# Third and fourth blocks of w3 and w_out converted as four units of 512 columns instead of two of 1024

## The chip, the cores and the metric

The program runs on one core of a Trainium2 chip. What counts is the device time of one execution in microseconds (us). The kernel before was timed three times: 809.39, 810.38 and 811.29 us, median 810.38 us. One further execution was recorded by the profiler; its own time was 810.48 us, and all rows below come from it.

## What is computed

The reference is a chain of a windowed attention and two layers on its result (2304 tokens, 512 wide). All inputs arrive as 64-bit floats.

```python
attn = softmax(mask(q @ k.T / 8, window=64)) @ v          # 4 x 8 heads, 576 tokens, 64 wide
x = attn as (2304, 512)
a = x @ w1;  b = x @ w2                                   # 512 -> 1024
h = (a * b) @ w3                                          # w3: 1024 x 1024
x = h @ w_out                                             # w_out: 1024 x 512
g = leaky(x @ w_in);  out = g @ w_out2                    # 512 -> 2048 -> 512
```

## The kernel before

The chip has no 64-bit floats, so every weight is loaded as raw words and turned into 32-bit floats on the core. One piece of a weight that goes through this is called a **unit** here. The list `units` (filled by `unit`, L503) holds them in the order in which they are loaded and converted. A unit passes through five steps, each one or two instructions:

1. load: SP starts a DMA into a raw buffer (`load_unit`, L418);
2. scale: ACT scales the high words (L455) and takes three low bits out of the low words (`low_bits`, L427);
3. shift: DVE shifts the high words and joins the low bits (L483);
4. bits: DVE puts the sign in (`sign`, L432). At this point the raw buffer is free, and `feed` may start the load of a later unit, whose field `after` says how many units must have passed this step;
5. fin: for a weight that is used as it is (w_out, w1, w2), `store` makes two parts of it: ACT rounds it into a high part (L357) and DVE or POOL subtracts that for the low part (L368 on DVE for the first w_out blocks, L361 on POOL for the third and fourth slot, L366 on POOL for w1 and w2). For w3 nothing is computed; its words wait in `words`.

`advance` does one such step for several units at a time, which makes a software pipeline; `until(n, ...)` runs it until n units are finished.

The first phase of the program multiplies w3 by w_out once, so that later only one matrix is needed (`wf`). The loop over `its` goes through 16 blocks: two halves `gi` of w3's rows, and in each eight blocks `l` of 128 columns. For each block PE transposes four 128 x 128 pieces of w3 (`w3_tr`, L517; the result is read out by ACT, L519, and DVE, L520, into the tile `w3T`), and multiplies them with block `l` of w_out (`w3_mm`: three products for each of four 128 x 512 results, L77, L78, L79, written into `mm`). `w3_tr` runs two blocks ahead of `w3_mm`. At the end of a half the four results are read out into `wf` (L540 on ACT, L541 on DVE).

The attention of the first chunk of tokens is interleaved with this phase, by slot numbers (`plan_att`, `slot`): loads of q, k and v (L670), transposes of k and q on PE (L235) with a read-out of k by ACT (`kT`, L242) and of q by DVE (`qbd`, L254), scores (L268), softmax (L272 on DVE, L276 on ACT, L284 and L285 on DVE, L286 on POOL), the transposes of the weights (L299, read out by ACT, L302) and the products with v (L331), which ACT and DVE read out into `x` (L334, L335). The tile `pa`, into which L235 and L331 both write, has one buffer, so a transpose of the next k waits until DVE's L335 has read the products.

The order on each engine is fixed when the program is built. A scheduler places the instructions by its own estimate of times, with priorities; small differences in the units change where it puts them. On the chip each engine works through its list in order.

Units before: 0 to 3 are w3 block 0, w_out block 0, w3 block 1, w_out block 1, each of 512 columns (512 KB). All others have 1024 columns (1024 KB): units 4 and 5 are blocks 2 and 3 of w3 together and of w_out together, and so on. Raw buffers are four slots of `raw_all`, and two tiles borrowed from `wf` (`wf_raw`).

Of the kernel before, what the change touches and what calls it, by code (L numbers as in the profile page):

```python
# [21 lines left out]
def tile_kernel(ctx: ExitStack, tc: tile.TileContext, q, k, v, w1, w2, w3, w_out, w_in, w_out2, out):  # L22
# [18 lines left out]
    P = 128  # L41
# [4 lines left out]
    KF = DFF // P  # L46
# [12 lines left out]
    UC = 512  # L59
# [9 lines left out]
    def f32(ap):  # L69
        return ap.bitcast(F32)  # L70

    def first():

        return tc.high_priority(offset=3000)
# [153 lines left out]
    def load(ls):  # L228
        for dst, src in ls:
            sp.dma_start(dst, src)  # L230
# [106 lines left out]
    def wslot(key):  # L337
        pl, tag, bufs = wpool, "w", 8
        if key[0] == "wo2":
            pl, tag, bufs = (po1, "w1", 4) if key[1] < 4 else (po2, "w2", 4)  # L340
        elif key[0] == "wf":
            tag, bufs = "wf", 4
        return pl.tile([P, 2, 2 * UC], F32R, name=tag, tag=tag, bufs=bufs)
# [7 lines left out]
    def store(key, half):  # L351

        def fin(f):
            if key not in slots:
                slots[key] = wslot(key)
            t, sl = slots[key], slice(0, 2 * UC) if half is None else slice(UC * half, UC * half + UC)
            act.copy(t[:, 0, sl], f)  # L357
            if key in (("wo", 2), ("wo", 3)):
                for i in range(2):
                    si = slice(UC * i, UC * i + UC)  # L360
                    pool.tensor_tensor(out=t[:, 1, si], in0=f[:, si], in1=f32(t[:, 0, si]), op=ALU.subtract)  # L361
                return
            if key[0] in ("w1", "w2"):
                for i in range(0, 2 * UC, 512):
                    si = slice(i, i + 512)
                    pool.tensor_tensor(out=t[:, 1, si], in0=f[:, si], in1=f32(t[:, 0, si]), op=ALU.subtract)  # L366
                return
            dve.tensor_tensor(out=t[:, 1, sl], in0=f, in1=f32(t[:, 0, sl]), op=ALU.subtract)  # L368
        return fin

    units = []
    last = {}
# [124 lines left out]
    def until(n, stop):  # L497
        while n_of["fin"] < n:
            was = dict(n_of)
            advance(stop)  # L500
            assert n_of != was

    def unit(src, fin, key, at=None, after=0, f_at=None):  # L503
        used = [(key[1], key[2] + j) for j in range(f_at[1])] if key[0] == "w3" else []
        units.append({"src": src, "fin": fin, "at": at, "after": after, "f_at": f_at,
                      "free": lambda: not any(x in words for x in used)})
        last[key] = len(units)
# [5 lines left out]
    def w3_tr(f):  # L513
        t = p0.tile([P, 2, 4, P], F32R, name="w3T", tag="w3T", bufs=2)
        ps = ps_ab.tile([P, 4, P], F32, name="ab", tag="ab")
        for i in range(4):
            pe.transpose(ps[:, i, :], f[:, i], ident)  # L517
        both = t.rearrange("p s i k -> p s (i k)")
        pss["act"] = act.copy(both[:, 0], ps.rearrange("p i k -> p (i k)")).ins  # L519
        pss["dve"] = dve.tensor_tensor(out=both[:, 1], in0=ps.rearrange("p i k -> p (i k)"), in1=f32(both[:, 0]),  # L520
                                       op=ALU.subtract).ins
        w3T.append(t)

    def w3_mm(gi, l, half):
        t = w3T[0]
        wo = rows2(slots["wo", l // 2])
        for i in range(2 * half, 2 * half + 2):
            if l == 0:
                wps[i] = ps_mm.tile([P, DM], F32, name="mm", tag="mm")
            mm3(wps[i], t[:, 0, i, :], t[:, 1, i, :], wo[:, 0, l % 2], wo[:, 1, l % 2], l == 0, l == KF - 1)  # L530
        if half == 0:
            return
        w3T.pop(0)
        if l == KF - 1:
            for i in range(2):
                if ("wf", 2 * gi + i) not in slots:
                    slots["wf", 2 * gi + i] = wslot(("wf", 2 * gi + i))
            for i in range(4):
                wf = rows2(slots["wf", 2 * gi + i // 2])
                act.copy(wf[:, 0, i % 2], wps[i])  # L540
                dve.tensor_tensor(out=wf[:, 1, i % 2], in0=wps[i], in1=f32(wf[:, 0, i % 2]), op=ALU.subtract)  # L541

    words = {}

    def wide_w3(gi, l):

        def fin(f):
            for j in range(2):
                words[gi, l + j] = f.rearrange("p (k j m) -> p k j m", j=2, m=P)[:, :, j]
        return fin  # L550

    def raw_at(i, n):
        return lambda: raw_all[:, i:i + n].rearrange("p n m -> p (n m)")
# [3 lines left out]
    def wf_raw(i):  # L557

        def at():
            if i not in spare_raw:  # L560
                spare_raw[i] = wpool.tile([P, 2 * UC], I64, name="wf", tag="wf", bufs=4)
            return spare_raw[i]
        return at

    for l in range(2):
        unit(w3[0:4 * P, P * l:P * l + P].rearrange("(k p) m -> p k m", p=P), (lambda l: lambda f: words.update({(0, l): f.rearrange("p (k m) -> p k m", m=P)}))(l),
             ("w3", 0, l), raw_at(2 * l, 1), 0, (2 * l, 1))
        unit(w_out[P * l:P * l + P, :], store(("wo", 0), l), ("wo", l), raw_at(2 * l + 1, 1), 0, (2 * l + 1, 1))
    PLACES = [wf_raw(0), wf_raw(1), raw_at(0, 2), raw_at(2, 2)]
    AFTER = {4: 0, 5: 0, 6: 2, 7: 4}  # L570
    for gi in range(2):
        for l in range(2 if gi == 0 else 0, KF, 2):
            i = len(units)
            unit(w3[4 * P * gi:4 * P * gi + 4 * P, P * l:P * l + 2 * P].rearrange("(k p) m -> p k m", p=P), wide_w3(gi, l),
                 ("w3", gi, l), PLACES[i % 4], AFTER.get(i, i - 3), (2 * (i % 2), 2))
            if gi == 0:
                i = len(units)
                unit(w_out[P * l:P * l + 2 * P, :].rearrange("(k p) m -> p k m", p=P), store(("wo", l // 2), None),
                     ("wo", l), PLACES[i % 4], AFTER.get(i, i - 3), (2 * (i % 2), 2))
    W12 = len(units)  # L580
    for p in range(KD):
        for w, name in ((w1, "w1"), (w2, "w2")):
            i = len(units)
            unit(w[:, 2 * P * p:2 * P * p + 2 * P].rearrange("(k p) m -> p k m", p=P), store((name, p), None), (name, p),
                 PLACES[2 + i % 2], i - 3 if i < W12 + 2 else i - 1, (2 * (i % 2), 2 if p else 0))
    PHASE_B = len(units)

    def keep(i):
# [54 lines left out]
    def slot():  # L643

        for _, n, _, f in sorted(ev.pop(clock["t"], []), key=lambda e: e[:2]):
            with ExitStack() as how:
                if f in (av, qk, tr) and clock["t"] >= PACED_FROM:
                    how.enter_context(tc.issue_after(pss["last"]))
                if f is prep_k and n > NHP or f is prep_q and n > 2 * NHP + 1:
                    how.enter_context(tc.issue_after(pss["dve"]))  # L650
                how.enter_context(tc.high_priority(offset=100))
                f(n)
        clock["t"] += 1
# [5 lines left out]
    def start_loads(i):  # L659

        if i in (W12 + 1, W12 + 2, W12 + 3):
            dma.append(pss["load"])
            for ls in held.pop(len(dma) - 1, []):
                with tc.issue_after(pss["load"]):
                    load(ls)
        for _ in range(0 if i < 5 else 1 if i < 10 else 7):
            if todo_qkv:
                dst, src = todo_qkv.pop(0)
                with tc.issue_after(pss["load"]), first():
                    pss["load"] = sp.dma_start(dst, src).ins  # L670
# [14 lines left out]
    for i, (gi, l) in enumerate(its):  # L685
        w3_mm(gi, l, 0)
        if i + 2 < len(its):
            g2, l2 = its[i + 2]
            if l2 % 2 == 0:
                until(last["w3", g2, l2], W12 + 2 if i >= 10 else W12)  # L690
            w3_tr(words.pop((g2, l2)))
            if l2 % 2 and g2 == 0:
                until(last["wo", l2 - 1], W12)
        for at, n in ((13, 1), (15, 2)):
            if i == at:
                until(W12 + n, W12 + 2)
        slot()
        w3_mm(gi, l, 1)
        slot()
# [220 lines left out]
    for c in range(NC):  # L920
        for i in range(3 * KF):
            f, part = divmod(i, 3)
# [357 lines left out]
```

## Time and profile before

| | |
|---|---|
| time of the three timed runs | 809.39, 810.38, 811.29 us; median 810.38 us |
| time of the profiled execution | 810.48 us |
| its span from the first to the last instruction | 808.7 us |
| mean granted clock of PE over the span | 0.998 of full speed |
| PE busy | 784.8 us (97%) |
| PE weight loads busy | 725.0 us (90%) |
| DVE busy | 560.8 us (69%) |
| ACT busy | 433.0 us (54%) |
| POOL busy | 71.4 us (9%) |

PE is the tensor engine, DVE the vector engine, ACT the scalar engine, POOL the general engine, SP the one that starts most DMAs. A busy time counts from the start of an instruction to its end. Since matmuls overlap, PE's busy share says only where PE has nothing at all to do. The granted clock is the share of full speed (2.4 GHz) that PE was given; 0.50 is 1.2 GHz.

### The profile page before, as it was taken

Reading aid. Unit: us, or ns where it says so; the run is one execution under the profiler, and the core shown is the slowest. Engines: PE = TensorE matmul, PEld = TensorE weight load, DVE = VectorE, ACT = ScalarE, POOL = GpSimd, SP = SyncE. Lnnn points to the kernel's source line nnn. Section 1 sums busy time; section 2 is a strip of 40 time slices with the busy share of each in tenths; the row PEclk is TensorE's granted clock in tenths of the full one; section 3 lists DMA queues with packets and bytes.
Section 4 is the critical chain, followed back from the end, with each engine's and each line's share of the span. In section 5 each row is a group of like instructions: output and inputs, shape, how many; then the busy total and the mean of one; then the engine's idle time right before and its main releaser. Section 6 shows DMA issues by size and latency. Waiting matters only on the chain.

```text
span 808.7 us, 14587 instructions
## 1 busy us (share of the span) xinstructions
PE 784.8 (97%) x5156; PEld 725.0 (90%) x5156; DVE 560.8 (69%) x1343; ACT 433.0 (54%) x968; POOL 71.4 (9%) x73
## 2 busy tenths in 40 slices
PE   5898999999999999999999999999999999999997
PEld 4776899999988888888788999999999999999997
DVE  6977676276446448884812865867668999898976
ACT  7885774244233325443511754654457867575744
POOL 1314244011011101110000000000000000000000
PEclk9999999999999999999999999999999999999999
DMA  9986374346646467894500557889998754444321
GB/s 338 301 252 160 103 204 113 82 114 150 158 109 166 102 157 197 261 292 160 180 8 1 170 191 272 287 320 338 319 314 285 216 166 135 128 139 130 111 92 53
DMA packets 184409, 147.12 MB, mean 182 GB/s; under 512 B 117904, under 2 KB 143760, under 8 KB 184336
## 3 DMA queue, kind: packets, MB, share of 16 engines
q1 hardware_dynamic: 181312, 141.34, 58.4%
q10 hardware_dynamic: 3024, 4.85, 1.6%
q8 instruction: 40, 0.66, 0.3%
q14 instruction: 33, 0.27, 0.1%
HBM read 98.96 MB, written 47.19 MB: 181 GB/s over the span
## 4 chain that ended last, share of the span: by engine, by line
PE 79%; DMA 7%; DVE 4%; SPq 3%; ACT 2%; issue 1%; POOL 0%; DVEq 0%; ACTq 0%; POOLq 0%
PE o L78 7%; PE o L79 7%; PE o L77 7%; PE pr L77 7%; PE pr L78 7%; PE pr L79 7%; PE ab L77 6%; PE ab L78 6%; PE ab L79 6%; PE mm L77 4%; PE mm L78 4%; PE mm L79 4%; PE sc L268 3%; SPq L230 3%; PE pa L331 2%; DMA wd<-f 2%
## 5 line engine op out<-in xcount | busy, mean ns | idle before, releaser
L77 PE MATMUL ab<-x,w 128*128 128x512 f32 (+1 forms) x320 | 119.6, 376 | 0.8 <-ACT a L719 0.8
L79 PE MATMUL ab<-x,w 128*128 128x512 f32 (+1 forms) x320 | 118.9, 371 | 0.0
L78 PE MATMUL ab<-x,w 128*128 128x512 f32 (+1 forms) x320 | 118.5, 370 | 0.0
L77 PE MATMUL pr<-yop,w 128*128 128x384 f32 x300 | 101.2, 337 | 1.0 <-ACT c L875 1.0
L79 PE MATMUL pr<-yop,w 128*128 128x384 f32 x300 | 101.0, 337 | 0.0
L78 PE MATMUL pr<-yop,w 128*128 128x384 f32 x300 | 100.9, 336 | 0.0
L875 ACT COPY c<-pr 128x384 f32<-128x384 f32 x95 | 45.2, 480 | 64.5 <-PE pr L79 55.9
L276 ACT ACTIVATE s<-s,nm 128x128 f32<-128x128 f32 x144 | 56.4, 395 | 39.3 <-DVE nm L272 38.8
L78 PE MATMUL o<-yop,yop 128*128 128x256 f32 x259 | 72.9, 282 | 0.0
L723 DVE TENSOR_TENSOR ab<-ab,a 128x512 f32<-128x512 f32 (+1 forms) x40 | 25.7, 642 | 68.2 <-PE ab L79 46.9
L79 PE MATMUL o<-yop,yop 128*128 128x256 f32 x259 | 72.9, 282 | 0.0
L77 PE MATMUL o<-yop,yop 128*128 128x256 f32 x259 | 72.9, 281 | 0.0
L77 PEld LDWEIGHTS ab<-x,w 128*128 128x128 f32 x320 | 60.1, 188 | 9.6 <-ACT a L719 1.5
L79 PEld LDWEIGHTS ab<-x,w 128*128 128x128 f32 x320 | 60.1, 188 | 8.0
L78 PEld LDWEIGHTS ab<-x,w 128*128 128x128 f32 x320 | 60.1, 188 | 7.6
L878 DVE TENSOR_TENSOR c<-pr,c 128x384 f32<-128x384 f32 x74 | 41.0, 555 | 29.9 <-PE pr L79 16.7
L1017 ACT CAST yop<-raw 128x256 fp32r<-128x256 f32 (+1 forms) x92 | 42.4, 485 | 35.6 <-PE o L78 34.2
L286 POOL TENSOR_TENSOR s<-s,rs 128x512 f32<-128x512 f32 (+1 forms) x40 | 39.5, 988 | 242.0 <-DVE rs L285 193.0
L78 PE MATMUL mm<-ab,wf 128*128 128x512 f32 (+1 forms) x160 | 60.4, 377 | 0.0
L79 PE MATMUL mm<-ab,wf 128*128 128x512 f32 (+1 forms) x160 | 59.5, 372 | 0.0
L77 PEld LDWEIGHTS pr<-yop,w 128*128 128x128 f32 x300 | 56.3, 188 | 1.7 <-ACT c L875 1.6
L724 ACT CAST ab<-ab 128x512 fp32r<-128x512 f32 (+1 forms) x40 | 21.7, 544 | 67.0 <-DVE ab L723 66.7
(148 smaller groups left out, 1981.4 us busy)
## 6 DMA issues: line engine op xcount, KB each, us to landing
hd<-c SPq DMA_DIRECT2D x96, 192.0 KB, 4.5
raw<-hd SPq DMA_DIRECT2D x32, 512.0 KB, 3.7
raw<-in_moe_w_dram SPq DMA_DIRECT2D x11, 1024.0 KB, 5.6
raw<-in_moe_w_out_dram SPq DMA_DIRECT2D x18, 512.0 KB, 5.0
raw<-in_moe_w_in_dram SPq DMA_DIRECT2D x16, 512.0 KB, 5.3
wd<-f SPq DMA_DIRECT2D x32, 256.0 KB, 4.3
raw<-wd SPq DMA_DIRECT2D x30, 256.0 KB, 4.8
pd<-tb SPq DMA_DIRECT2D x12, 512.0 KB, 2.8
```

The source lines that it names most:

```text
L77: pe.matmul(ps, lhsT=lh, rhs=rh, start=first, stop=False, skip_group_check=more)
L78: pe.matmul(ps, lhsT=lh, rhs=rl, start=False, stop=False, skip_group_check=more)
L79: return pe.matmul(ps, lhsT=ll, rhs=rh, start=False, stop=last, skip_group_check=more).ins
L230: sp.dma_start(dst, src)
L268: pe.matmul(sc[:, t, :], lhsT=qb[:, t, :], rhs=kT[n][:, k0:k0 + P], start=True, stop=True)
L276: act.activation(out=s[:, t, :], in_=s[:, t, :], func=AF.Exp, bias=nm[:, t:t + 1], scale=-1.0, accum_out=sm[:, t:t + 1])
L286: pool.tensor_tensor(out=s[:, 0:m], in0=s[:, 0:m], in1=rs[:, 0:m].unsqueeze(2).to_broadcast([P, m, P]), op=ALU.mult)
L723: dve.tensor_tensor(out=ps, in0=ps, in1=pss["a"], op=ALU.mult)
L724: pss["act"] = act.copy(t[:, 0], ps).ins
L875: pss["copy"] = act.copy(self.sb[to], ps).ins
L878: pss["add"] = dve.tensor_tensor(out=self.sb[to], in0=self.ps[at], in1=self.sb[of or to], op=ALU.add).ins
L1017: tied("act", lambda: act.copy(out, x))
```

## The change

Blocks 2 and 3 of w3 and of w_out for the first half now go through as four units of 512 columns, in the order w3 block 2, w_out block 2, w3 block 3, w_out block 3. They are loaded into halves of the two borrowed tiles (`wf_half`), where before each whole tile took one unit of 1024 columns. The list has two units more, so all later numbers rise by two: `PLACES` and `AFTER` are adapted, so that unit 8 (blocks 4 and 5 of w3) goes into the raw slots of units 0 and 1 as unit 6 did before. The counts at which loads of q, k and v start follow too. In the loop, `until` is now also called for the odd block 3.

A piece of w3 of 512 columns is four pieces of 128 columns next to each other, 1 KB of each row of the input; the piece of 1024 columns took 2 KB of each row. Rows of w_out are 4 KB in both.

```diff
-    for l in range(2):
-        unit(w3[0:4 * P, P * l:P * l + P].rearrange("(k p) m -> p k m", p=P), (lambda l: lambda f: words.update({(0, l): f.rearrange("p (k m) -> p k m", m=P)}))(l),
-             ("w3", 0, l), raw_at(2 * l, 1), 0, (2 * l, 1))
-        unit(w_out[P * l:P * l + P, :], store(("wo", 0), l), ("wo", l), raw_at(2 * l + 1, 1), 0, (2 * l + 1, 1))
-    PLACES = [wf_raw(0), wf_raw(1), raw_at(0, 2), raw_at(2, 2)]
-    AFTER = {4: 0, 5: 0, 6: 2, 7: 4}
+    def wf_half(i):
+        return lambda: wf_raw(i // 2)()[:, UC * (i % 2):UC * (i % 2) + UC]
+
+    for l in range(4):
+        half = (lambda i: raw_at(i, 1)) if l < 2 else wf_half
+        i = 2 * l % 4
+        unit(w3[0:4 * P, P * l:P * l + P].rearrange("(k p) m -> p k m", p=P),
+             (lambda l: lambda f: words.update({(0, l): f.rearrange("p (k m) -> p k m", m=P)}))(l), ("w3", 0, l), half(i), 0, (i, 1))
+        unit(w_out[P * l:P * l + P, :], store(("wo", l // 2), l % 2), ("wo", l), half(i + 1), 0, (i + 1, 1))
+    PLACES = [raw_at(0, 2), raw_at(2, 2), wf_raw(0), wf_raw(1)]
+    AFTER = {8: 2, 9: 4, 10: 6, 11: 8}
     for gi in range(2):
-        for l in range(2 if gi == 0 else 0, KF, 2):
+        for l in range(4 if gi == 0 else 0, KF, 2):
...
-                 PLACES[2 + i % 2], i - 3 if i < W12 + 2 else i - 1, (2 * (i % 2), 2 if p else 0))
+                 PLACES[i % 2], i - 3 if i < W12 + 2 else i - 1, (2 * (i % 2), 2 if p else 0))
...
-        for _ in range(0 if i < 5 else 1 if i < 10 else 7):
+        for _ in range(0 if i < 7 else 1 if i < 12 else 7):
...
-            if l2 % 2 == 0:
+            if ("w3", g2, l2) in last:
                 until(last["w3", g2, l2], W12 + 2 if i >= 10 else W12)
             w3_tr(words.pop((g2, l2)))
-            if l2 % 2 and g2 == 0:
-                until(last["wo", l2 - 1], W12)
+            if g2 == 0 and (l2 % 2 or l2 < 4):
+                until(last["wo", l2 if l2 < 4 else l2 - 1], W12)
```

Two places show what this does to the lists of the engines. The first is DVE near the start, from the low part of w_out block 0 on. In a row, what is written stands left of the arrow and what is read right of it; `f_99` holds the words in work, `raw_98`, `wf_123`, `wf_125` and `wf_126` are raw buffers, `w_100` and `w_101` the slots of w_out. Before:

```order
L368 TENSOR_TENSOR w_100<-f_99,w_100 128x512
L483 SCALAR_TENSOR_TENSOR f_99<-raw_98 128x512
L432 SCALAR_TENSOR_TENSOR f_99<-raw_98,f_99 128x512
L483 SCALAR_TENSOR_TENSOR f_99<-wf_123 128x1024
L520 TENSOR_TENSOR w3T_187<-ab_188,w3T_187 128x512
L368 TENSOR_TENSOR w_100<-f_99,w_100 128x512
L432 SCALAR_TENSOR_TENSOR f_99<-wf_123,f_99 128x1024
L483 SCALAR_TENSOR_TENSOR f_99<-wf_125 128x1024
L432 SCALAR_TENSOR_TENSOR f_99<-wf_125,f_99 128x1024
```

And now, from the same instruction on:

```order
L368 TENSOR_TENSOR w_100<-f_99,w_100 128x512
L483 SCALAR_TENSOR_TENSOR f_99<-raw_98 128x512
L483 SCALAR_TENSOR_TENSOR f_99<-wf_123 128x512
L432 SCALAR_TENSOR_TENSOR f_99<-raw_98,f_99 128x512
L432 SCALAR_TENSOR_TENSOR f_99<-wf_123,f_99 128x512
L483 SCALAR_TENSOR_TENSOR f_99<-wf_123 128x512
L520 TENSOR_TENSOR w3T_189<-ab_190,w3T_189 128x512
L368 TENSOR_TENSOR w_100<-f_99,w_100 128x512
L432 SCALAR_TENSOR_TENSOR f_99<-wf_123,f_99 128x512
L483 SCALAR_TENSOR_TENSOR f_99<-wf_126 128x512 x2
```

The shift of w3 block 2 has moved ahead of the sign step of w_out block 1, and shift and sign of a unit no longer follow each other directly.

The second place is PE about 70 us into the span, in the second half of w3, where the transposes of k for the last pair of heads (`pa_693` before, `pa_705` now) wait for DVE to free `pa`. `ab_...` are transposes of attention weights (`s_...`) or of w3 (`f_99`), `sc_...` scores, `mm_...` the products with block 4 of w_out. Before:

```order
L235 MATMUL pa_693<-ident_94,x_117 128x128 x3
L235 MATMUL pa_723<-ident_94,x_117 128x128 x2
L299 MATMUL ab_717<-ident_94,s_609 128x128 x3
L517 MATMUL ab_743<-ident_94,f_99 128x128 x4
L268 MATMUL sc_754<-kT_692,qbd0_96 128x128 x3
L235 MATMUL pa_796<-ident_94,x_117 128x128 x2
L517 MATMUL ab_780<-ident_94,f_99 128x128 x4
L77 MATMUL mm_618<-w_102,w3T_742 128x512
```

Now:

```order
L235 MATMUL pa_705<-ident_94,x_117 128x128 x3
L299 MATMUL ab_729<-ident_94,s_621 128x128 x3
L517 MATMUL ab_755<-ident_94,f_99 128x128 x4
L235 MATMUL pa_735<-ident_94,x_117 128x128 x2
L517 MATMUL ab_792<-ident_94,f_99 128x128 x4
L77 MATMUL mm_630<-w_102,w3T_754 128x512
L78 MATMUL mm_630<-w_102,w3T_754 128x512
L77 MATMUL mm_634<-w_102,w3T_754 128x512
```

The transposes of q (`pa_735`) now come after seven other transposes, and the products `mm_630` come before the scores (`sc_766` follows them). The twelve products of the block before, which stood directly ahead of `pa_693`, now stand further ahead: what stands directly ahead of `pa_705` is the products with v (L331) that fill `pa`.

## Rows read from the trace of the kernel before

**Rows 1.** Busy time by stretch: stretch, us, then busy time and count of each engine.

```profile
core 0: us, PE busy (x) PEld busy (x) DVE busy (x) ACT busy (x) POOL busy (x), PEclk, DMA share, GB/s
...
20.00:30.00 10.00, 7.56 (x36) 5.94 (x37) 9.84 (x11) 8.91 (x12) 1.57 (x1) 1.00 1.09 370
...
60.00:70.00 10.00, 7.82 (x59) 5.85 (x57) 9.92 (x23) 6.79 (x18) 3.25 (x2) 1.00 0.46 94
...
100.00:110.00 10.00, 10.00 (x79) 9.65 (x80) 7.55 (x18) 7.55 (x14) 5.40 (x5) 1.00 0.63 191
```

**Rows 2.** PE in order of time: start, us, instruction, [idle before, releaser].

```profile
21.99 1.20 PE L77 MATMUL mm<-w,w3T 128*128 128x512 f32 x4 [2.14 <-ACT w L357]
```

**Rows 3.** The chain that ended last, 24 to 31 us: start, us, what.

```profile
24.71 1.24 DVE f L483
25.97 1.24 DVE f L432
27.23 1.06 ACT w L357
28.43 2.33 POOL w L361
30.81 1.21 PE mm L78 x4
```

**Rows 4.** ACT in order of time, first 18 us.

```profile
4.65 0.65 ACT L455 ACTIVATE raw<-raw 128x512 f32<-128x512 f32 x1 [2.63 <-DMA raw<-in_moe_w_dram]
5.21 0.64 ACT L427 ACTIVATE raw<-raw 128x512 int32<-128x512 uint8 x1
...
7.77 0.68 ACT L455 ACTIVATE raw<-raw 128x512 f32<-128x512 f32 x1 [0.54 <-DMA raw<-in_moe_w_dram]
...
11.82 1.18 ACT L455 ACTIVATE wf<-wf 128x1024 f32<-128x1024 f32 x1 [0.68 <-DMA wf<-in_moe_w_dram]
12.88 1.16 ACT L427 ACTIVATE wf<-wf 128x1024 int32<-128x1024 uint8 x1
13.91 0.59 ACT L519 CAST w3T<-ab 128x512 fp32r<-128x512 f32 x1
...
17.39 1.20 ACT L455 ACTIVATE raw<-raw 128x1024 f32<-128x1024 f32 x1 [0.30 <-DMA raw<-in_moe_w_dram]
```

**Rows 5.** DVE in order of time, 11 to 16 us.

```profile
11.44 0.68 DVE L483 SCALAR_TENSOR_TENSOR f<-raw 128x512 int32<-128x512 int32 x1
...
14.07 1.22 DVE L483 SCALAR_TENSOR_TENSOR f<-wf 128x1024 int32<-128x1024 int32 x1 [1.21 <-ACT wf L427]
15.21 0.68 DVE L520 TENSOR_TENSOR w3T<-ab,w3T 128x512 fp32r<-128x512 f32 x1
15.81 0.68 DVE L368 TENSOR_TENSOR w<-f,w 128x512 fp32r<-128x512 f32 x1
```

**Rows 6.** DVE in order of time, 67 to 70 us.

```profile
67.20 1.20 DVE L284 TENSOR_SCALAR rs<-sm 128x3 f32<-128x3 f32 x1
68.32 1.21 DVE L432 SCALAR_TENSOR_TENSOR f<-wf,f 128x1024 int32<-128x1024 int32 x1
69.45 0.55 DVE L335 TENSOR_TENSOR x<-pa,x 128x384 fp32r<-128x384 f32 x1
```

**Rows 7.** POOL in order of time, 65 to 69 us.

```profile
65.12 3.25 POOL L366 TENSOR_TENSOR w<-raw,w 128x512 fp32r<-128x512 f32 x2 [9.16 <-ACT w L357]
```

**Rows 8.** PE in order of time, 70 to 76 us.

```profile
70.05 0.55 PE L235 MATMUL pa<-ident,x 128*128 128x128 f32 x3 [2.04 <-DMA vt<-in_v_dram]
71.17 0.44 PE L235 MATMUL pa<-ident,x 128*128 128x128 f32 x2 [0.57 <-ACT kT L242]
72.27 0.68 PE L299 MATMUL ab<-ident,s 128*128 128x128 f32 x3 [0.66 <-POOL s L286]
```

**Rows 9.** Granted clock by half microsecond; columns as in rows 1.

```profile
72.50:73.00 0.50, 0.50 (x5) 0.50 (x4) 0.01 (x1) 0.00 (x0) 0.50 (x2) 0.54 1.05 382
...
75.50:76.00 0.50, 0.50 (x6) 0.50 (x4) 0.50 (x7) 0.43 (x3) 0.01 (x1) 0.55 0.36 58
```

## The prediction

> **What bounds the kernel now.** I read the busy time by stretch first, because a mean over the span hides where PE is short of work. From 100 us on PE is busy all the time [rows 1] and DVE has room, so an instant lost or won before that moves everything behind it by about as much. PE's idle time lies in the first 80 us. In the stretches 20 to 30 us and 60 to 70 us PE is busy 7.56 and 7.82 of 10 us, DVE 9.84 and 9.92 [rows 1]: there DVE, which converts the weights, sets the pace, and PE's work is fitted around it.
>
> Then I read the places where PE stands. The first is 2.14 us before 21.99 [rows 2], where the products of w3 block 2 wait for ACT's high part of w_out block 2. The second is in the chain that ended last, 24 to 31 us [rows 3]: the shift and the sign step of w_out blocks 4 and 5 on DVE, ACT's rounding, POOL's subtraction, PE. The third is at 68 to 72.3 us [rows 8]: 2.04 us, then 0.57 for the read-out of k, then 0.66 for POOL. The trace writes the 2.04 us down to a DMA, but DVE's rows tell it otherwise: the transposes of k write into `pa`, which DVE's L335 frees at 69.45 + 0.55 = 70.00 us [rows 6], and PE starts at 70.05. L335 stood behind a sign step and behind a subtraction on 128x3 that took 1.20 us [rows 6], while POOL was in its two subtractions for w1 [rows 7]. After this sparse stretch the granted clock is at 0.5 (1.2 GHz) from about 72.5 to 76 us [rows 9], so of 3.5 us of work another 1.7 us is lost. Together 2.04 + 0.57 + 0.66 + 1.7 = 5.0 us hang on this one place, more than on the start.
>
> **The loads.** ACT's first instruction on a unit waits for its load at 4.65, 7.77, 11.82 and 17.39 us [rows 4]; these are the landings of units 0, 2, 4 and 6, and they follow each other as fast as the queue moves. Between the last two lie units 5 and 6 (2 MB and a little of k) in 5.57 us, 1.35 us for 512 KB. Between 7.77 and 11.82 lie unit 3 and unit 4 (1.5 MB) in 4.05 us, again 1.35. Between 4.65 and 7.77 lie one 512 KB unit of w_out and one of w3 in 3.12 us: the piece of w3 with runs of 1 KB takes 3.12 - 1.35 = 1.77 us. The change makes two more such pieces, so the loads behind them land 2 x 0.42 = 0.85 us later: the new units 4 to 7 at 7.77 + 1.35 + 1.77 = 10.9, 12.2, 14.0 and 15.4 us, and unit 8 (unit 6 before) at 17.39 + 0.85 = 18.2. Unit 4 lands 0.9 us earlier than the whole piece did. What hides the later landing of unit 8 is that ACT reaches it only at 17.8 us (below); without that cover it would cost up to 0.85 us.
>
> **The instructions.** On ACT two halves of 512 start 0.56 us apart (4.65 and 5.21), a whole of 1024 takes 1.06 (11.82 and 12.88) [rows 4]: a split costs 0.06 us. On DVE 1.14 (14.07 to 15.21) becomes twice 0.60 (15.21 to 15.81) [rows 5], again 0.06. Five instructions are split on either engine (two scale, two low bits and one rounding; two shifts, two signs and one subtraction): 0.3 us each. Against this, shift and sign of 1024 that follow each other directly stand 1.26 us apart (24.71 and 25.97) [rows 3] and not 1.14; in the new order other work is between them, which gives back about 0.2 us.
>
> **The start.** ACT takes unit 4 when it has landed, at 11.0 us, and has 4 and 5 done by 11.0 + 4 x 0.57 = 13.3, two roundings by 14.3 (one took 0.59 from start to end [rows 4], and the next starts sooner), units 6 and 7 by 16.7, two more roundings by 17.8. DVE's shift of unit 4 can start at 12.3 and not at 14.07, so of its 1.21 us of idle time [rows 5] some 0.3 is left: 0.9 won, 0.3 paid for the splits, 0.2 won back. The sign step of w_out blocks 4 and 5, which ended at 27.2 us [rows 3], then ends at about 26.4: **0.8 us** earlier. ACT's rounding behind it gains less, some 0.3 us, as two roundings of transposed w3 now stand ahead of it; PE has by then done the first scores and a transpose of q, which it had not before. So the 2.14 us of rows 2 don't vanish; a wait of about 1.2 us for the first `qbd` and one for POOL take their place. I take DVE's 0.8 us, since DVE stays the engine with least room up to 70 us; the bounds are 0 (its lead is lost in its own later waits) and 2.1 (all of the idle time of rows 2).
>
> **The order at 70 us.** The new order puts seven transposes between those of k and of q, and the eight products of block 4 ahead of the scores. While ACT reads out k and POOL scales the weights, PE has that work to do: the 0.57 and 0.66 us of rows 8 should be covered, **1.2 us**. The cover is gone if the read-out of w3 on ACT is late as well. The wait before it doesn't shrink by itself: the twelve products that stood directly ahead of it are done earlier now, so it is longer to look at, but it still ends when L335 ends. The bounds are 0 and the whole 5.0 us of the place, if L335 comes early enough that PE neither stands nor drops to 1.2 GHz; nothing in the new order suggests that, so I stay near the lower row.
>
> **The sum.** 810.48 - 0.8 - 1.2 = 808.5 us for the profiled execution; it was 0.1 us above the median, so **808.4 us**. Past 100 us I take the orders as equal in cost: the same instructions, moved by a few places, on a PE that is always busy.
>
> **The rivals.** First, nothing that can be told: the start gains 0.3 us behind ACT's roundings and the idle time at 70 us comes back in another form (a DVE subtraction held up for 1.1 us, 1.20 instead of about 0.1, as in rows 6, eats the rest). For it speaks that the wait at 70 us is set by DVE, POOL and the one buffer of `pa`, none of which the change touches. Time 810.0 us.
>
> Second, the place at 70 us dissolves: 810.4 - 5.0 = 805.4 us. For it speaks that it took an unlucky hold-up of 1.1 us on DVE (rows 6, 7) that depends on where POOL's subtraction falls; against it, that the twelve products no longer stand ahead of it.
>
> Third, slower: the stretch without work at 66 to 70 us gets longer, because the twelve products are gone from it. If L335 comes 1.1 us later than before (POOL's subtraction holds DVE up once more), PE stands close to 5 us, and the slow clock lasts for twice as long, 1.7 us more; with the 0.8 us of the start already in L335's time this is +1.1 + 1.7 - 0.8 = +2.0, 812.4 us. It decides from L335 ending later than about 71 us.
>
> Fourth, the loads cost more than I say. The units of 512 KB of w3 took 1.77 us against 1.35 [rows 4], those of w_out did not. If all four halves went at 1.77, unit 8 would land at 19.1 us, ACT would stand for more than 1 us and the sign step of the chain would end 0.8 us later, where it ended before: 809.2 us. The Trainium skill (DMA: Bandwidth & Descriptors, Bandwidth) has a rule that speaks for this one: batch DMAs to at least 1 MiB, because smaller ones reach a smaller share of the peak. By that rule all four halves would be slower; rows 4 show it for w3 alone, where the runs are shorter, and not for the size.
>
> **How the numbers follow.** About 0.2%, 1.6 us, is what a measurement of this kernel can tell from no change. My forecast has 0.42; nothing to tell 0.25; the place dissolves 0.13; slower 0.12; the loads 0.08. Of the forecast's 0.42 its bounds leave some 0.08 within 0.2%. Faster by over 0.2%: 0.34 + 0.13 = 0.47. Within: 0.25 + 0.08 + 0.08 = 0.41. Slower: 0.12. The range goes from the second rival, 805.2, to just above the timed runs, 811.4, and leaves out most of the third rival and a little below.
>
> **What would show it.** Unit 4's scale at about 11.0 us and unit 8's at 18.2 or sooner; DVE's shift of unit 4 near 12.3 with little idle time; the sign step of w_out blocks 4 and 5 ending at 26.4; L335 of the third pair of heads at 69.2 or sooner, then the transposes of k, and the products of block 4 starting near 72 us where they started at 76. Wrong would be a first block of waits at 20 to 30 us as long as before with DVE idle in it, or a half clock that lasts past the place it had.

## The result and the profile after

The changed kernel took **818.54 us** (median of 4, 818.30 to 818.81) where the kernel before, timed beside it, took 810.84 us: a ratio of 1.0084, 95% interval 1.0064 to 1.0103 (the two medians alone give 1.0095, inside it). It is slower by 0.84%, where 808.4 us was forecast and the range ended at 811.4. The profiled execution (818.81 us, span 817.0) is 8.3 us longer than the one of before.

**The start came as forecast.** These rows answer to [rows 3 to 5]: ACT's scale steps (L455) on the new units, the shift of unit 4 on DVE, and the sign step of w_out blocks 4 and 5.

```profile
10.96 0.68 ACT L455 ACTIVATE wf<-wf 128x512 f32<-128x512 f32 x1
17.58 1.18 ACT L455 ACTIVATE raw<-raw 128x1024 f32<-128x1024 f32 x1
12.23 0.69 DVE L483 SCALAR_TENSOR_TENSOR f<-wf 128x512 int32<-128x512 int32 x1 [0.18 <-ACT wf L427]
25.27 1.23 DVE L432 SCALAR_TENSOR_TENSOR f<-raw,f 128x1024 int32<-128x1024 int32 x1
```

And PE in the stretch from 26 to 32 us:

```profile
27.18 0.94 PE L268 MATMUL sc<-kT,qbd 128*128 128x128 f32 x6 [1.04 <-DVE qbd L254]
29.60 0.50 PE L78 MATMUL mm<-w,w3T 128*128 128x512 f32 x1 [0.34 <-POOL w L361]
```

Unit 4 was taken at 10.96 us (forecast 11.0), unit 8 at 17.58 without a wait for its load, DVE stood 0.18 us where it had stood 1.21, and the sign step ended at 26.50 (forecast 26.4, before 27.2). The wait of 2.14 us [rows 2] is gone; 1.04 us for `qbd` and 0.34 us for POOL stand in its place.

**The place at 70 us got worse.** DVE, with POOL beside it, and PE; the rows answer to [rows 6 to 8].

```profile
68.54 1.78 DVE L432 SCALAR_TENSOR_TENSOR raw<-raw 128x1024 int32<-128x1024 int32 x1
70.33 0.52 DVE L335 TENSOR_TENSOR x<-pa,x 128x384 fp32r<-128x384 f32 x1
67.95 3.53 POOL L366 TENSOR_TENSOR w<-raw,w 128x512 fp32r<-128x512 f32 x2 [12.06 <-ACT w L357]
70.91 0.90 PE L235 MATMUL pa<-ident,x 128*128 128x128 f32 x3 [2.88 <-DVE x L335]
72.32 0.90 PE L299 MATMUL ab<-ident,s 128*128 128x128 f32 x3 [0.51 <-POOL s L286]
```

The windows of 10 us, which answer to [rows 1] (busy us and number of instructions of PE, PEld, DVE, ACT, POOL; granted clock; DMA share, GB/s):

```profile
60.00:70.00 10.00, 6.96 (x52) 4.92 (x50) 9.85 (x24) 7.37 (x19) 2.05 (x2) 0.97 0.38 71
70.00:80.00 10.00, 8.58 (x41) 7.49 (x42) 5.97 (x19) 4.50 (x11) 5.57 (x5) 0.69 0.75 176
100.00:110.00 10.00, 6.93 (x25) 6.64 (x26) 7.77 (x13) 5.23 (x9) 5.00 (x5) 0.67 0.48 151
```

And the first half microsecond that is wholly at half clock, which answers to [rows 9] (PE busy and its instructions, clock, DMA):

```profile
69.50:70.00 0.50, 0.00 (x0) 0.50 0.31 50
```

It begins some 3 us sooner than before (72.5), while PE still waits, and lasts to about 76 us as before.

**And a new stall stands at 98 to 110 us**, where PE had been busy all the time [rows 1]: 6.93 of 10 us, at a mean granted clock of 0.67. The timeline of PE there (start, duration, what; in brackets the wait and who ended it):

```profile
95.43 0.57 PE L331 MATMUL pa<-pts,x 128*64 128x64 f32 x12
98.23 0.62 PE L77 MATMUL ab<-x,w 128*128 128x384 f32 x2
101.42 0.52 PE L299 MATMUL pa<-ident,s 128*128 128x128 f32 x3 [2.58 <-DVE x L335]
104.28 0.69 PE L77 MATMUL ab<-x,w 128*128 128x384 f32 x1 [1.65 <-ACT a L724]
108.29 1.48 PE L77 MATMUL mm<-ab,wf 128*128 128x384 f32 x4
109.57 0.52 PE L77 MATMUL ab<-x,w 128*128 128x384 f32 x1
```

What it waits for, on ACT and DVE:

```profile
95.77 2.02 ACT L540 CAST wf<-mm 128x512 fp32r<-128x512 f32 x4
97.66 0.51 ACT L334 CAST x<-pa 128x384 fp32r<-128x384 f32 x1
102.81 1.05 ACT L357 CAST w<-f 128x1024 fp32r<-128x1024 f32 x1 [0.29 <-DVE f L432]
103.76 0.47 ACT L724 COPY a<-ab 128x384 f32<-128x384 f32 x1
98.33 2.48 DVE L541 TENSOR_TENSOR wf<-mm,wf 128x512 fp32r<-128x512 f32 x4
100.73 0.55 DVE L335 TENSOR_TENSOR x<-pa,x 128x384 fp32r<-128x384 f32 x1
```

In the kernel before, at the same place, on ACT, DVE and PE:

```profile
93.85 0.45 ACT L334 CAST x<-pa 128x384 fp32r<-128x384 f32 x1
94.21 1.52 ACT L540 CAST wf<-mm 128x512 fp32r<-128x512 f32 x3
94.86 0.55 DVE L335 TENSOR_TENSOR x<-pa,x 128x384 fp32r<-128x384 f32 x1
97.14 1.85 DVE L541 TENSOR_TENSOR wf<-mm,wf 128x512 fp32r<-128x512 f32 x3
92.89 0.57 PE L331 MATMUL pa<-pts,x 128*64 128x64 f32 x12
98.39 0.49 PE L299 MATMUL pa<-ident,s 128*128 128x128 f32 x3
99.88 0.44 PE L77 MATMUL ab<-x,w 128*128 128x384 f32 x1 [0.30 <-ACT a L719]
102.77 0.33 PE L77 MATMUL ab<-x,w 128*128 128x384 f32 x1
```

This is where the first phase hands over to the second. The products of attention's fourth pair of heads (L331) end in `pa`; ACT and DVE read them out as `x` (L334, L335). The last products of the first `ab` group need that `x` (those at 98.23 us its high part, those behind the transposes its low part), and the next pair's transposes (L299) need the buffer. At the same time the finished w3 x w_out products wait to be read out into `wf` (L540, L541), which nobody needs until the `mm` products at 108 us. Before, `x` went first on both engines. In the changed program the four read-outs of `wf` stand ahead of it on both, 2.0 and 2.5 us, and `x` is complete at 101.28 us, 5.9 us later than before (95.41). PE's first `ab` group begins 1.2 us *earlier* than before (93.65 against 94.89) and its third one 6.8 us later (109.57 against 102.77).

Two waits (2.58 and 1.65 us), and then the granted clock is at 0.50 (the lower of the two levels, 1.2 GHz) from about 103.5 to 110 us: twelve `ab` products and four of `mm` take 109.57 - 104.28 = 5.3 us, before 102.77 - 99.88 = 2.9 us.

The 8.3 us add up from PE's idle time and what the low clock costs (busy time x (1 - granted clock), taken by half microseconds, since a mean clock over 10 us counts time in which PE stands). Idle: 1.0 us less before 60 us, 1.0 more from 60 to 80, 3.9 more from 90 to 110, 0.4 more from 110 to 320, 0.4 more behind that. Clock: 0.7 us more at 69 to 76 (2.4 against 1.7), 3.0 more at 103 to 110. The sum is 8.4 us. Part of the 0.4 us from 110 to 320 is a new wait of 1.63 us at 207 us, for a DMA that loads `pts`; before, 0.93 us at 126 and 0.28 us at 199 stood in that stretch.

### The profile page after: what moved, and what is told of

Its sections match the earlier page's. It is cut to its first block, busy times and chain, and to the rows that moved or that the text cites. A ratio compares the mean times of both kernels' runs of the same rounds, so it can differ in the third digit from the quotient of the medians.

```text
span 817.0 us, 14609 instructions
## 1 busy us (share of the span) xinstructions
PE 788.4 (96%) x5156; PEld 727.9 (89%) x5156; DVE 562.3 (69%) x1348; ACT 433.4 (53%) x973; POOL 69.2 (8%) x73
## 4 chain that ended last, share of the span: by engine, by line
PE 87%; DVE 4%; DMA 3%; ACT 2%; SPq 1%; issue 1%; POOL 1%; DVEq 0%; ACTq 0%; POOLq 0%
PE ab L77 8%; PE ab L78 8%; PE ab L79 8%; PE o L78 7%; PE o L79 7%; PE o L77 7%; PE pr L77 7%; PE pr L79 7%; PE pr L78 6%; PE mm L77 5%; PE mm L78 5%; PE mm L79 5%; PE sc L268 3%; PE pa L331 2%; DVE f L432 1%
## 5 line engine op out<-in xcount | busy, mean ns | idle before, releaser
L77 PEld LDWEIGHTS ab<-x,w 128*128 128x128 f32 x320 | 60.7, 190 | 11.3 <-ACT a L724 2.9
L79 PEld LDWEIGHTS ab<-x,w 128*128 128x128 f32 x320 | 60.8, 190 | 8.0
L78 PEld LDWEIGHTS ab<-x,w 128*128 128x128 f32 x320 | 60.8, 190 | 7.9 <-DVE x L335 0.3
```

Of the source, the lines that this page charges most:

```text
L77: pe.matmul(ps, lhsT=lh, rhs=rh, start=first, stop=False, skip_group_check=more)
L78: pe.matmul(ps, lhsT=lh, rhs=rl, start=False, stop=False, skip_group_check=more)
L79: return pe.matmul(ps, lhsT=ll, rhs=rh, start=False, stop=last, skip_group_check=more).ins
```

## The experiments

**Theory A**: the loss is this order at the hand-over and the slow clock behind it. **Rival B**: the four smaller units cost by themselves, through their loads and instructions. **Rival C**: it is the place at 70 us with its clock. Each ratio is to the kernel before, run in turn on the same chip; its median was 811.80 us beside experiments 1 (first time), 2 (first test) and 3, 811.36 us beside 2 (second test), 4 and 5, and 811.91 us beside 1 (second time) and 6.

**1. x first again.** The changed kernel, with only this:

```diff
-        act.copy(x[:, 0, 0:W * m], pa)
-        dve.tensor_tensor(out=x[:, 1, 0:W * m], in0=pa, ...)
+        pss["xh"] = act.copy(x[:, 0, 0:W * m], pa).ins
+        pss["xl"] = dve.tensor_tensor(out=x[:, 1, 0:W * m], in0=pa, ...).ins
...
+                    if gi == 1:
+                        how.enter_context(tc.issue_after(pss["xh"]))
+                        how.enter_context(tc.issue_after(pss["xl"]))
                     act.copy(wf[:, 0, i % 2], wps[i])
```

> The changed kernel with one order put back: the read-outs of the last w3 x w_out products into wf (ACT's casts, DVE's subtractions) are issued behind the read-out of x of the fourth pair of heads, as in the kernel before. Theory A (the loss is this order: PE stood 2.58 us for x and 1.65 us for the read-out of the first ab product, and then ran at 0.50 of the clock from 104 to 110 us): both waits shrink to under 0.5 us each, the granted clock is 1.00 from 100 to 110 us, and the time falls by 2.2 + 1.3 + 2.8 = 6.3 us to about 812.2 us (811.0 to 813.5). Rival B (the four smaller units themselves cost the time, by their loads and instructions): it stays at 816.5 or more. Rival C (the stall at 68 to 71 us with its slow clock carries the loss): it stays above 816 with 2.9 us of wait at 70 us.

Measured: 813.27 us, ratio 1.0024 (1.0012 to 1.0036). The kernel was run once more, and the profile is taken from there.

> The kernel of e1 once more, for a profile at full clock (that of e1 fell into a disturbed execution): theory A wants the waits at 98 to 104 us, 2.58 and 1.65 us in the changed kernel, below 0.5 and below 1.1 us, no half clock from 104 to 110 us, and a time of 811 to 814 us. What is left above the kernel before should be seen either at 68 to 72 us (2.9 us of wait and a low clock) or at 200 to 208 us (1.6 us for a DMA of pts).

Measured: 814.16 us, ratio 1.0027 (1.0014 to 1.0040). PE at the hand-over:

```profile
99.53 0.52 PE L299 MATMUL pa<-ident,s 128*128 128x128 f32 x3 [0.36 <-DVE x L335]
101.86 0.44 PE L77 MATMUL ab<-x,w 128*128 128x384 f32 x1 [1.11 <-ACT a L728]
105.09 0.98 PE L77 MATMUL mm<-ab,wf 128*128 128x384 f32 x4 [0.85 <-ACT ab L733]
```

The clock is 1.00 from 100 to 110 us. One order, with the split untouched, gives back 0.57 to 0.60 of the 0.84%, some 4.8 us; the expected 6.3 did not come in full, because ACT's read-outs of `ab` are still late by 1.11 and 0.85 us. B and C wanted 816 us or more. What is left, 0.25%, is about 2 us. In the trace PE stands idle 2.0 us longer than in the kernel before at 90 to 112 us and 1.3 us longer at 60 to 80 us (where its wait for `x` is still 2.89 us).

**2. The same order in the kernel before.** No split; `x`'s read-out is held until wf's are issued, and PE, POOL and the load queue keep their order.

```diff
+        if n == NHP - 1:
+            held_x.append(read)
...
+            if gi == 1:
+                with tc.issue_after(pss["wh"]), tc.issue_after(pss["wl"]), ...:
+                    held_x.pop()()
```

> The kernel before, without any split, with one order changed: the read-out of x of the fourth pair of heads is issued behind the four wf read-outs on ACT and DVE; PE's, POOL's and the load queue's orders are as they were. Theory A: DVE's subtraction for x starts near 99.0 us instead of 94.86, PE's transposes into pa wait about 1.1 us where they waited nothing, the products behind wait up to another 1 us for ACT; with the clock held that is 811.9 to 812.8 us, and with a drop to half of it up to 815. Rival B: no difference from the kernel before, 810.8 us within 0.2%.

Measured: 811.63 us, ratio 1.0016 (0.9998 to 1.0034), which can't be told from no change. `x` was read out at 97.63, not 99.0, and PE waited 0.59 us for it, at a clock of 1.00. DVE was not as far behind there as in the changed kernel, so the test was too weak. (Three of the twelve runs took 814.47 to 815.87 us, longer than any of the 29 of the kernel before beside it, at most 812.98; the profiled one took 810.06, so no trace shows why.) The next one makes up for it: four more subtractions of 2.5 us in all (wf's low parts written again) ahead of `x`.

```diff
+                for i in range(4):
+                    with tc.issue_after(pss["wl"]):
+                        ...
+                        pss["wl"] = dve.tensor_tensor(out=wf[:, 1, i % 2], in0=wps[i], ...).ins
```

> The kernel before, unsplit, as in e2, with four more DVE subtractions of 128x512 (wf's low parts written a second time, 2.5 us) ahead of the subtraction for x. It then starts at about 100.1 us, near the 100.73 of the changed kernel. Theory A with the size of the changed kernel: PE waits 2.5 to 3 us for x, another 1 to 1.7 us for the read-out of the first ab product, the clock falls to 0.50 for some 6 us: 815 to 819 us. If a late x costs only its own wait and the clock holds: 813.3 to 814.5 us. Rival B: no difference from the kernel before.

Measured: 815.99 us, ratio 1.0053 (1.0033 to 1.0074). PE, and then the windows behind the wait (PE busy and its instructions, granted clock, DMA):

```profile
104.18 0.88 PE L299 MATMUL pa<-ident,s 128*128 128x128 f32 x3 [2.98 <-DVE x L336]
```

```profile
102.00:104.00 2.00, 0.00 (x0) 0.86 1.04 402
104.00:106.00 2.00, 1.82 (x7) 0.50 0.22 84
106.00:108.00 2.00, 2.00 (x7) 0.50 0.00 0
```

A late `x`, in a kernel without any split, costs 0.53%, 4.3 us; the 2.5 us of added subtractions that make it late are part of the test. In the profiled execution, 817.07 us, it is 2.98 us of wait for `x` where that kernel had none, and 3.0 us by the half clock that the rows show behind it. That is more than the 4.3 us; the four runs go from 813.08 to 817.32 us, and whether the clock fell in each isn't shown. The second wait, for ACT, didn't come: the added work stood on DVE only.

**3. One half of the split at a time.**

w3 only, and then w_out only (the places of the later units move up by one):

```diff
+    for l in range(2, 4):
+        unit(w3[0:4 * P, P * l:P * l + P]..., ("w3", 0, l), wf_half(l - 2), 0, (l - 2, 1))
+    unit(w_out[2 * P:4 * P, :]..., store(("wo", 1), None), ("wo", 2), wf_raw(1), 0, (2, 2))
```

```diff
+    unit(w3[0:4 * P, 2 * P:4 * P]..., wide_w3(0, 2), ("w3", 0, 2), wf_raw(0), 0, (0, 2))
+    for l in range(2, 4):
+        unit(w_out[P * l:P * l + P, :], store(("wo", 1), l % 2), ("wo", l), wf_half(l), 0, (l, 1))
```

> Only w3's third and fourth blocks are loaded and converted as two units of 512 columns; w_out's two stay one unit of 1024. In the order that results, wf's four read-outs stand ahead of x's of the fourth pair, as in the changed kernel. Theory A: PE waits 1 to 3 us for x near 100 us and the time is 813.5 to 818.5 us. Rival B (each split costs its share): about half of the loss, 814.7 us, without such a wait. Rival C: the time goes with the wait at 70 us and its clock.

> Only w_out's third and fourth blocks are loaded and converted as two units of 512 columns; w3's two stay one unit of 1024. In the order that results, x's read-out of the fourth pair stands ahead of wf's, as in the kernel before. Theory A: no wait of over 0.5 us near 100 us, clock 1.00 there, 809 to 811.5 us. Rival B: about half of the loss, 814.7 us. Rival C: the time goes with the wait at 70 us and its clock.

Measured: w3 only 815.97 us, ratio 1.0059 (1.0040 to 1.0078); w_out only 811.72 us, ratio 0.9998 (0.9987 to 1.0009). PE at the hand-over, first with w3 only, then with w_out only:

```profile
99.50 0.62 PE L77 MATMUL ab<-x,w 128*128 128x384 f32 x2 [2.73 <-ACT x L334]
101.78 0.87 PE L299 MATMUL pa<-ident,s 128*128 128x128 f32 x3 [1.66 <-DVE rs L285]
```

```profile
101.06 0.45 PE L77 MATMUL ab<-x,w 128*128 128x384 f32 x1 [0.30 <-ACT a L725]
```

Which of the two is slow follows from the order at the hand-over, as A said, and not from the number of pieces. Rival C falls here as well: the slow one has no wait for x at 70 us and a clock of 1.00 from 60 to 80, the unharmed one waits 3.38 us there, at a clock of 0.83. (Its 811.72 us lies 0.2 us above the range of its forecast, which was drawn from a kernel before at 810.8.)

**4. The slow half, x first.** The first diff, on the kernel with w3 split only.

> The kernel with only w3 split (e3), with x's read-out of the fourth pair ahead of wf's. Theory A: the waits of 2.73 us at 99.5 and 1.66 us at 101.8 go, and with them the half clock of 100 to 110 us (about 3 us): 816.0 - 7 = 809 us (808 to 811), at or below the kernel before, since the place at 70 us lost only 0.6 us in e3. Rival B: half of the split's cost stays, 814 us or more.

Measured: 811.44 us, ratio 1.0000 (0.9987 to 1.0012): the order gives back all of it. The forecast of 809 failed, since waits of 0.80 and 1.70 us stayed at 98 to 102 us, and one of 1.60 us at 83.9 was now followed by a half clock (below).

**5. The place at 70 us, too.** One sign step moved behind a later `x` read-out, with x first at the hand-over; on the changed kernel and on the kernel before.

```diff
+            with tc.issue_after(pss["xl"]) if now["bits"] == W12 + 1 else nullcontext():
                 sign(f, u["hi"])
```

> The changed kernel with x's read-out of the fourth pair put ahead of wf's, as in e1, and besides one sign step on DVE (that of the first piece of w2, 1.78 us at 68.54 in the changed kernel, directly ahead of the x subtraction that frees pa at 70.85) issued behind a later x subtraction. If the place at 70 us is what is left of the loss after e1, the subtraction ends 1.8 us sooner, the wait of 2.88 us before the transposes of k falls to about 1.1 us and the clock stays higher: 1.8 to 3 us less than e1, 810.3 to 811.5 us. If what is left is the split's own cost, it stays at e1's 813.3 us within 0.2%.

> The kernel before with the same two orders laid down: wf's read-outs behind x's of the fourth pair (as they are already), and the sign step of the first piece of w2 out of the place at 70 us. There it stood at 68.32 for 1.1 us, so the x subtraction ends 1.1 us sooner and the wait of 2.04 us falls to 0.9: 1.1 to 2.8 us less than the kernel before, 808 to 810 us. Against the run before this one it gives the worth of the split under like orders: about -0.8 us (split faster) if the start's gain of 0.7 us is kept, 0 if it is lost on the way, +1.5 or more if the split itself costs.

Measured: changed kernel 812.65 us, ratio 1.0020 (1.0007 to 1.0033); kernel before 814.19 us, ratio 1.0028 (1.0014 to 1.0043). PE in the changed kernel, and then in the kernel before:

```profile
70.24 0.55 PE L235 MATMUL pa<-ident,x 128*128 128x128 f32 x3 [1.18 <-DVE x L335]
99.35 0.44 PE L77 MATMUL ab<-x,w 128*128 128x384 f32 x1 [1.82 <-ACT a L729]
```

```profile
70.54 0.69 PE L235 MATMUL pa<-ident,x 128*128 128x128 f32 x3 [2.03 <-DVE x L335]
102.17 0.69 PE L77 MATMUL ab<-x,w 128*128 128x384 f32 x1 [3.73 <-ACT a L724]
```

In the changed kernel the wait at 70 us fell to 1.18 us as expected, with the clock at 1.00 from 60 to 80, and yet the time hardly moved: PE came to the hand-over sooner, conversions of w1 and w2 stood there ahead of ACT's read-out of `a` (from 95.47 to 98.57 us), and PE waited 1.82 us with a half clock behind. That is not all that this trace loses (815.01 us, the longest of the twelve runs): at 202 us PE waited 2.03 us for the DMA that loads `pts`, and the half clock behind cost 1.7 us more.

In the kernel before, the edit missed its aim. The sign step that it moves, that of w2's first piece, stood behind the subtraction for `x` there already:

```profile
69.92 1.21 DVE L432 SCALAR_TENSOR_TENSOR raw<-raw 128x1024 int32<-128x1024 int32 x1
```

The step at 68.32 us [rows 6], which the forecast took for it, belongs to the last piece of w3. So the wait at 70 us stayed at 2.03 us, w2's piece came later, PE waited 3.73 us at the hand-over, and the time rose by 0.28%. The worth of the split under like orders can't be read from this pair. What the pair does show is that a shorter wait at 70 us did not shorten the time while the hand-over was late.

**6. The hand-over cleared.** x first, and besides the steps of w1's and w2's later pieces written behind the product of their place, their rounding on ACT behind the last read-out of `ab`; on all three kernels.

```diff
+            with tc.issue_after(pss["copy"]) if "copy" in pss and key[0] in ("w1", "w2") else nullcontext():
                 act.copy(t[:, 0, sl], f)
...
-                if part < 2:
-                    advance(PHASE_B)
...
                 ab_step(c, f, part)
+                if c == 0:
+                    advance(PHASE_B)
```

> The changed kernel with x's read-out ahead of wf's (e1), and with the conversion of the later pieces of w1 and w2 kept out of the way where the phase begins: each of their steps is written behind the product of its place, not ahead of it, and ACT's rounding of such a piece is issued behind the last read-out of ab. Theory A: with the critical read-outs first, no wait of over 0.5 us stands at 93 to 110 us and the clock is 1.00 there: 1 to 2 us below e1, 811 to 812 us. If the pieces then come late for their products, waits for w1 or w2 behind 105 us eat that up: 813 us or more.

> The same two edits on the kernel with only w3 split (e7 plus the cleared place). e7 lost 0.8 + 1.7 us at 98 to 102 us; with these gone and the rest as in e7 it is 811.4 - 2.5 = 809 us (808 to 810.5), faster than the kernel before. If pieces of w1 or w2 come late: 811 us or more.

> The same two edits on the kernel before, unsplit. It had only 0.3 us of wait there and its x was first already, so 0 to 0.9 us less (its wait of 0.9 us near 126 us may go too): 810.3 to 811.4 us. Against the changed kernel under the same edits it tells what the split is worth where the orders are alike: 0.7 us faster for the split if the start's gain reaches the end, equal if it doesn't, over 1.5 us slower if the split costs by itself.

Measured: changed kernel **810.51 us, ratio 0.9987** (0.9974 to 0.9999); w3 only 815.61 us, 1.0048 (1.0030 to 1.0066); kernel before 813.25 us, 1.0021 (1.0006 to 1.0035). PE in the changed kernel (its only wait from 92 to 320 us) and DVE there, and then PE in the kernel with only w3 split:

```profile
100.07 0.44 PE L77 MATMUL ab<-x,w 128*128 128x384 f32 x1 [0.71 <-ACT a L729]
96.85 0.55 DVE L335 TENSOR_TENSOR x<-pa,x 128x384 fp32r<-128x384 f32 x1
97.32 2.47 DVE L546 TENSOR_TENSOR wf<-mm,wf 128x512 fp32r<-128x512 f32 x4
```

```profile
122.23 1.65 PE L77 MATMUL mm<-ab,wf 128*128 128x384 f32 x4 [3.14 <-ACT ab L736]
```

With the hand-over clear the split loses nothing: the kernel is 0.13% below the kernel before, less than the 0.2% that can be told. Against experiment 1's trace PE stands 1.6 us less at 90 to 112 us, and 1.5 us less behind that, since waits for DMAs at 201 and 214 us are gone too; no run shows whether those hang on the same order. Rival B is out: three kernels with the split or with half of it are no slower than the kernel before (0.9998, 1.0000, 0.9987). The comparison under the same edits says less than the forecast hoped. By it the whole split would gain 2.7 us (813.25 - 810.51), and w3's half alone would cost 2.4 us (815.61 - 813.25). The same edits left each kernel with waits of its own: w3 only got the 3.14 us shown, and in the kernel before, where the hand-over shows 0.30 us of wait with or without them, it stays open where 0.2% went. An order is good for one kernel, not in general.

## Why the prediction was wrong

**The step that failed** is one sentence: "Past 100 us I take the orders as equal in cost: the same instructions, moved by a few places, on a PE that is always busy." It put at nothing what measured 3.9 + 3.0 = 6.9 us at the hand-over. That PE was busy all the time [rows 1] was a property of the old order, in which `x` was read out 3 us before PE needed it, and not of the work. The order of the changed kernel was there to be read, with wf's read-outs ahead of x's. And the prediction had told at 70 us what happens when a subtraction for `x` stands behind conversions and `pa` has one buffer; it didn't ask where else that buffer changes hands. Why the planned order came out so is not shown by any run; that it turns with small edits is (w3 only has it, w_out only has not).

**The start** (forecast -0.8) was right in each instant and in size (27.2 - 26.5 = 0.7 us). Instants of two executions are to be compared with care: in three kernels with one order up to here the transposes at 70 us began at 70.05, 69.40 and 71.70 us, with ACT's third bit step at 8.35, 7.90 and 9.33. Counted from that step they began at 61.7, 61.5 and 62.4 us (the last after a half clock near 26 us that the other two don't have). In the changed kernel the sign step came 0.6 us sooner by this count than in the profile of before, and the transposes at 62.65 us, 0.95 us later. So the start's gain was spent before 71 us.

**The order at 70 us** (forecast -1.2) had the wrong sign: idle time +1.0 and clock +0.7 us. The covers worked in part (0.57 for the read-out of k is gone, POOL's 0.66 became 0.51), but the wait ahead grew from 2.04 to 2.88 us. This is the third rival's mechanism at 1.7 us where it gave 1.1 + 1.7 = 2.8. The half clock did last twice as long, 69 to 76 us against 72.5 to 76, but PE stood for much of the added time. No products stand ahead, and DVE was held up once more, a sign step of 1.78 us beside POOL's subtractions where 1.22 is usual. Its mark, L335 later than about 71 us, was nearly met (70.85). L335 is the second subtraction for `x`; the prediction called it the third pair's.

**The loads** were no cost: nothing after 7.68 us waits for a weight's load on ACT up to unit 8. Unit 8 had landed by 17.58 us where the forecast gave 18.2, so the 0.42 us that it charged for each smaller piece of w3 were too much. The fourth rival, all four halves at 1.77 us and unit 8 at 19.1, is out by the same row. The rule of the Trainium skill that it cites (DMA: Bandwidth & Descriptors, Bandwidth) is to batch DMAs to at least 1 MiB; no loss from the loads of 512 KB shows in this trace.

**The rivals** held no case for the end of the phase, and the chance of slower, 0.12, was priced from the one mechanism at 70 us; even that rival ended at 812.4 us. In a program whose order is set anew by every edit, a change in the first 30 us can cost anywhere that a single buffer or an engine's queue decides.

## What to carry to other kernels

Where an edit moves instructions, look first at the places where a phase hands over: list which read-outs the next products and the next user of a single buffer wait for, and see in the new order whether anything that nobody needs yet stands ahead of them. A PE that is busy in the old trace has no reserve by that; measure the reserve as the time between the read-out's end and the product's start. And when an edit comes out slower, put back the one order before judging the edit: here that turned +0.84% into +0.25%, and clearing the hand-over into -0.13%, no loss that can be told (though the same clearing left the kernel with only w3 split at +0.48% and the kernel before at +0.21%).

## What the runs showed of the hardware

A wait of the same length is sometimes followed by the lower clock and sometimes not. PE stands for 1.60 us before the same scores at 83.7 to 83.9 us in two of the kernels with only w3 split. The first window is from experiment 3, where the granted clock stays at 1.00; the second from experiment 4, where it is at half until about 88 us (PE busy and its instructions, clock, DMA). In the kernel with only w3 split of experiment 6 the same wait of 1.60 us was followed by half the clock until about 91 us, which cost 3.4 us.

```profile
86.00:87.00 1.00, 1.00 (x19) 1.00 0.00 0
```

```profile
86.00:87.00 1.00, 1.00 (x16) 0.50 0.00 0
```

The same holds near 25 us for one order of instructions: in the profile of before PE stood 2.14 us [rows 2] and the clock stayed at 1.00; in the second test of experiment 2, which has that order up to there, it stood 2.01 us before the same products, and the clock was at half from about 25 to 28 us. The row is from that test, then a window of before and one of that test.

```profile
22.86 1.20 PE L77 MATMUL mm<-w,w3T 128*128 128x512 f32 x4 [2.01 <-ACT w L365]
```

```profile
25.00:26.00 1.00, 1.00 (x6) 1.00 1.09 318
```

```profile
26.00:27.00 1.00, 1.00 (x5) 0.50 1.08 335
```

The one wait of 1.82 us in experiment 5 was followed by half the clock from about 101 to 104 us, while 0.36, 1.11 and 0.85 us within 6 us in experiment 1 left it at 1.00. So a stand of PE near 2 us had two prices in these runs, its own length, and now and then 1.7 to 3.4 us more by the half clock behind it, and a forecast has to carry both.
